# Putting float64 weights together as float32 with one multiplication and two bit operations

## The chip, the core and the metric

The kernel runs on one core of a Trainium2 chip. The metric is the device time of one execution in microseconds (us), the median of several runs. The core has five engines with a queue of instructions each, executed in the order of the program: TensorE (PE), VectorE (DVE), ScalarE (ACT), GpSimd (POOL) and SyncE (SP). DMA transfers run beside them.

## What is computed

The reference is an attention over a small state, a mixture of experts in which each row takes one expert, and a dense feed-forward layer (FFN) on the result:

```python
def _moe_ref(x, expert_emb, tau, w1, w2):          # x: 4352 rows (B*S+Ns rows of attention) of 512
    ...                                            # routing: expert_idx = argmax of cosine logits, gate_w = its softmax value
    for e in range(8):
        mask = expert_idx == e
        h = np.maximum(x[mask] @ w1[e], 0.0)       # w1[e]: 512 x 1024
        out[mask] = gate_w[mask, None] * (h @ w2[e])

def _moe2_ref(x, w_in, w_out):                     # w_in: 512 x 2048, w_out: 2048 x 512
    h = x @ w_in
    relu6 = np.clip(h + 3.0, 0.0, 6.0)
    g = h * relu6 / 6.0
    return (g @ w_out).astype(np.float32)
```

`w1` and `w2` come as float32. `w_in` and `w_out` are drawn as float32 and multiplied by `1.0 / np.sqrt(...)`, a float64 number, so they arrive as **float64**: each value is a pair of 32-bit words. The output is float32.

## The kernel before

The kernel splits every float32 operand of its large products into a high half, rounded to PE's float32r format, and a low half, what the rounding left; a product is then three matmuls (high by high, high by low, low by high). Four stretches follow one another, with overlap:

- **Attention**, up to some 130 us: eight batches, each with its scores, exponentials and products, whose results `xr` go to a DRAM buffer.
- **Routing**, to some 145 us: the logits `lg` of all rows, their argmax, a rank of each row within its expert, and from that the tiles (slots) of 128 rows.
- **Experts**: a lead part (a unit of four slots and a single one), then units of two slots and of one. For each, rows are fetched, transposed (`xq`) and split (`xt`); expert weights are loaded as `raw` and split into `wh` (a cast) and `wl` (a subtraction, L1249); `h_ps` is the first product (L1410), `hx` its split Relu, `y_ps` or `y_g` the second product (L1513); the result rows go to the DRAM buffer `ysd` by way of tiles `yt`.
- **FFN**: 17 blocks of 256 rows. A block's rows are read back and split into `yh` and `yw`; then sixteen times F1 (`u_ps`, L1619, weights `wih` and `wil`) and F2 (`o`, L1654, weights `woh` and `wol`). Between them `r` is a Relu on ACT with a bias of three (L1623), then a product with the smaller of `r` and 6 on DVE, and its split into `gh` and `gl`. At a block's end the two accumulators are scaled by 1/6 (L1668, L1670) and stored. Blocks of the FFN run among the expert units.

**The conversions.** The float64 weights become float32 in 32 conversions (`Conv`), one for every 128 x 512 chunk: sixteen chunks of `w_in` (m = 0 to 15, `i`) and sixteen of `w_out` (`o`). A chunk is loaded as pairs of words by a DMA that ACT issues; `low` and `top` are views of every second word of that buffer. Seven instructions follow: on ACT `cv` (L295), a Relu over the upper 16 bits of the lower word, that leaves a small integer in `low`; on DVE `ca` (L303, L304), which shifts the upper word and takes its sign and exponent bits together in `cv_m`; on ACT `cq` (L312), a Square of the upper word read as a float; on DVE `cb` (L308), which puts the small integer into the last bits, and `cp` (L316), which multiplies by zero where the square is below a bound; then the split, `ch` (L324, ACT, a copy into the high half) and `cl` (L327, the subtraction for the low half, on POOL or DVE).

The first 14 conversions take their buffers from a pool of their own (`cv_raw` and `cv_m`, two of each). The last 18 take the raw buffer from the FFN's tiles `yh` and `yw`, and `cv_m` from the pool of rows ("row", six buffers), which the tiles `yt` and the output rows use as well. In the trace such a conversion therefore reads `cv_m<-yh`.

**What sets the order.** A planner (`Sched`) runs while the program is built. Every step of the kernel is an operation with a cost for each engine, a due time (`prio`), the operations that it depends on, and the ring of buffers from which it takes (`hold`) and gives back. The planner appends, one after another, the operation that can begin earliest by its own reckoning, with the due time weighed in, and so fixes the order of every engine's queue. A conversion of an FFN weight is due 36.654 planner microseconds ahead of the F1 or F2 that first needs it (L1779 to L1786). In `convert` the raw buffer (`hr`) is taken by the load and `cv_m` (`hc`) by `ca`; both are given back after `cl`.

Of the kernel before, what the change touches and what calls it, by code (L numbers as in the profile page):

```python
# [8 lines left out]
F32 = mybir.dt.float32  # L9
F32R = mybir.dt.float32r  # L10
BF16 = mybir.dt.bfloat16
I32 = mybir.dt.int32
U16 = mybir.dt.uint16
AF = mybir.ActivationFunctionType
ALU = mybir.AluOpType
# [139 lines left out]
def kernel(  # L155
# [13 lines left out]
    PE, ACT, DVE, POOL, SP = nc.tensor, nc.scalar, nc.vector, nc.gpsimd, nc.sync  # L169
# [97 lines left out]
    class Conv:  # L267
# [4 lines left out]


        def __init__(self, w, m):
            self.w, self.m = w, m
            src = w_in if w == "i" else w_out
            self.wide = src.dtype != F32
            self.src, self.n = (src.bitcast(I32), 2) if self.wide else (src, 1)

        def load(self, pool):  # L280
# [7 lines left out]
            if self.wide:  # L288
                v = t.rearrange("p (f w) -> p f w", w=2)
                self.low, self.top = v[:, :, 0], v[:, :, 1]  # L290

        def cv(self):

            if self.wide:
                ACT.activation(self.low, self.raw.bitcast(U16).rearrange("p (f w) -> p f w", w=4)[:, :, 1], AF.Relu,  # L295
                               bias=seven[:, 0:1], scale=-(2.0**-13))

        def ca(self, pool):
            self.ma = self.raw
            if self.wide:  # L300
                t = self.bits = pool().bitcast(I32)
                self.ma = t.bitcast(F32)
                DVE.tensor_scalar(t, self.top, 3, 0x3FFFFFFF, op0=ALU.logical_shift_left, op1=ALU.bitwise_and)  # L303
                DVE.scalar_tensor_tensor(t, self.top, -0x40000000, t, op0=ALU.bitwise_and, op1=ALU.bitwise_or)  # L304

        def cb(self):
            if self.wide:
                DVE.scalar_tensor_tensor(self.bits, self.low, 7, self.bits, op0=ALU.bitwise_xor, op1=ALU.bitwise_or)  # L308

        def cq(self):  # L310
            if self.wide:
                ACT.activation(self.top.bitcast(F32), self.top.bitcast(F32), AF.Square)  # L312

        def cp(self, e="P"):
            if self.wide:
                eng[e].scalar_tensor_tensor(self.ma, self.top.bitcast(F32), (1.0625 * 2.0**-15)**2, self.ma,  # L316
                                            op0=ALU.is_ge, op1=ALU.mult)

# [11 lines left out]
    last_conv, dense = [None], {}  # L330

    def convert(n, prio, pool, ma, gate=None, start=0.0):

# [5 lines left out]
        a.ready = start  # L339
        v = op(c.cv, {"A": 0.55}, prio, [a])  # L340
        b = op(lambda: c.ca(ma), {"D": 0.96}, prio, [a], [hc], port="D")
        q = op(c.cq, {"A": 0.55}, prio, [b])
        b = op(c.cb, {"D": 0.61}, prio, [b, v], port="D")
        f = op(lambda: c.cp("D"), {"D": 0.6}, prio, [b, q], port="D")
        g = op(c.ch, {"A": 0.55}, prio, [f, home])
        dense[conv_q[n]] = op(*((lambda: c.cl("P"), {"P": 1.26}) if early else (c.cl, {"D": 0.6, "P": 1.26})), prio, [g], (), [hr, hc], port="DP")
        if early:
# [827 lines left out]
    pool = {}  # L1175
# [432 lines left out]
    def F1(i, m, prio, deps=()):  # L1608
# [12 lines left out]
        def ra():  # L1621
            q["r"] = pool["ffn"].tile([128, 256], F32, tag="r", name="r")
            ACT.activation(q["r"], q["p"], AF.Relu, bias=pool["three"][:, 0:1])  # L1623

# [17 lines left out]
    def F2(i, m, prio, deps=()):  # L1642
# [18 lines left out]
        for a in range(2):  # L1661
# [3 lines left out]
            def scale(a=a, box=box):  # L1665
                t = box["t"] = pool["row"].tile([128, W], F32, tag="row", name="yo")[:, 0:DM]
                if a:
                    DVE.tensor_scalar(t, o["o"][1], 1.0 / 6, None, op0=ALU.mult)  # L1668
                else:
                    ACT.activation(t, o["o"][0], AF.Copy, scale=1.0 / 6)  # L1670

# [201 lines left out]
```

## Time and profile before

| | |
|---|---|
| median of 3 runs | 1447.35 us |
| the runs | 1445.01, 1447.35, 1447.62 us |
| the profiled execution, its own time | 1445.17 us |
| its span (first to last instruction) | 1443.5 us |
| mean granted clock of TensorE | 0.961 of full speed |
| bytes read from and written to HBM | 146.09 MB, 27.82 MB |

The profile is of one execution of the program; its time lies within the runs. A page of it gives the busy time of each engine, and the same in 40 slices of the span (36 us each). Behind the page stands the trace, from which busy times of single stretches, waits with the instruction that ended them, and single instructions in order of time are read. PEclk is the TensorE clock that was granted, as a share of full speed: 1 is 2.4 GHz, 0.5 is 1.2 GHz. PE is the matmuls, PEld the weight loads that overlap them.

### The profile page before, as it was taken

What the parts mean: (1) busy time and instruction counts of PE and PEld (TensorE: products, weight loads), DVE (VectorE), ACT (ScalarE), POOL (GpSimd) and SP (SyncE); (2) the same over time, 40 slices, a digit from 0 to 9 for tenths busy, and PEclk for the clock granted to TensorE, in tenths of its full rate; (3) what the DMA queues carried; (4) which work ended last, traced back from release to release, by engine and by line L of the source; (5) the groups of instructions that cost most, each with busy time, mean ns of one, the idle gap of its engine ahead of it and who ended that gap; (6) DMA issues with size and microseconds to landing.
All of it is one profiled execution on the core that took longest, in us unless ns stands there. A gap on an engine that the chain in (4) does not pass through costs nothing. (4 is left out here: it accounts for less than half of the span.)

```text
span 1443.5 us, 24914 instructions
## 1 busy us (share of the span) xinstructions
PE 1349.8 (94%) x8912; PEld 1194.9 (83%) x8912; DVE 907.5 (63%) x2102; ACT 588.5 (41%) x1276; POOL 421.0 (29%) x445
## 2 busy tenths in 40 slices
PE   7985797877899999999999999999999999999997
PEld 5764676775789899888989898998989999899996
DVE  6987876978865555545555545777756676434332
ACT  4764524555433243433334343333434444323332
POOL 4432546313252241413133133333333311100000
PEclk8997788999899999999999999999999999999999
DMA  6654336556454333333324233554545544101000
GB/s 161 182 168 144 123 103 179 181 169 189 132 176 145 106 102 112 112 109 97 117 89 125 89 111 110 161 154 159 163 135 156 167 142 152 46 23 30 15 16 15
DMA packets 151762, 175.60 MB, mean 122 GB/s; under 512 B 43784, under 2 KB 116488, under 8 KB 150608
## 3 DMA queue, kind: packets, MB, share of 16 engines
q1 hardware_dynamic: 128544, 121.19, 28.0%
q0 software_dynamic: 12336, 35.99, 8.2%
q10 hardware_dynamic: 10752, 16.78, 3.6%
q8 instruction: 71, 1.16, 0.3%
q14 instruction: 59, 0.48, 0.1%
HBM read 146.09 MB, written 27.82 MB: 120 GB/s over the span
## 5 line engine op out<-in xcount | busy, mean ns | idle before, releaser
L1619 PE MATMUL u_ps<-yh,wih 128*128 128x256 f32 x1088 | 305.6, 281 | 1.0 <-PEq L1828 0.9
L1619 PE MATMUL u_ps<-yw,wih 128*128 128x256 f32 x1088 | 305.7, 281 | 0.5 <-DVE yw L1598 0.5
L1619 PE MATMUL u_ps<-yh,wil 128*128 128x256 f32 x1088 | 305.2, 281 | 0.0
L1623 ACT ACTIVATE r<-u_ps,three 128x256 f32<-128x256 f32 x272 | 129.0, 474 | 347.5 <-PE u_ps L1619 343.3
L1626 DVE SCALAR_TENSOR_TENSOR u_ps<-r,u_ps 128x256 f32<-128x256 f32 x272 | 116.4, 428 | 223.4 <-ACT r L1623 223.1
L1654 PE MATMUL o<-woh,gh 128*128 128x512 f32 x544 | 216.7, 398 | 1.6 <-DVE yo L1668 1.3
L1654 PE MATMUL o<-wol,gh 128*128 128x512 f32 x544 | 215.9, 397 | 0.0
L1619 PEld LDWEIGHTS u_ps<-yh,wih 128*128 128x128 f32 x1088 | 205.7, 189 | 10.8 <-DVE gl L1633 2.2
L1654 PE MATMUL o<-woh,gl 128*128 128x512 f32 x544 | 214.4, 394 | 0.0
L1619 PEld LDWEIGHTS u_ps<-yw,wih 128*128 128x128 f32 x1088 | 205.0, 188 | 8.7 <-DVE yw L1598 0.7
L1619 PEld LDWEIGHTS u_ps<-yh,wil 128*128 128x128 f32 x1088 | 205.6, 189 | 0.0
L1249 DVE TENSOR_TENSOR wl<-raw,wh 128x512 fp32r<-128x512 f32 x272 | 191.1, 712 | 9.2 <-ACT wh L1246 4.7
L1630 ACT CAST gh<-u_ps 128x256 fp32r<-128x256 f32 x272 | 101.3, 372 | 211.7 <-PE o L1654 168.7
L1633 DVE TENSOR_TENSOR gl<-u_ps,gh 128x256 fp32r<-128x256 f32 x272 | 114.8, 422 | 112.7 <-ACT gh L1630 112.3
L1513 PE MATMUL y_ps<-wh,hx 128*128 128x512 f32 x512 | 184.5, 397 | 0.0
L1249 POOL TENSOR_TENSOR wl<-raw,wh 128x512 fp32r<-128x512 f32 x80 | 109.5, 1369 | 252.2 <-DVE wh L1246 122.8
L1277 POOL DMA_INDIRECT xq<-xd,qidx x128 | 130.4, 1018 | 79.0 <-DVE xt L1330 44.0
L1410 PE MATMUL h_ps<-xt,wh 128*128 128x256 f32 x704 | 145.9, 297 | 0.8 <-ACT wh L1246 0.6
L1246 DVE CAST wh<-raw 128x512 fp32r<-128x512 f32 x232 | 100.6, 436 | 63.2 <-PE y_ps L1513 23.0
L1410 PE MATMUL h_ps<-xt,wl 128*128 128x256 f32 x352 | 105.6, 300 | 27.8 <-DVE wl L1249 23.0
L1673 POOL DMA_INDIRECT out_dram<-yo,ix x34 | 37.5, 1104 | 311.1 <-DVE yo L1668 215.7
L1410 PEld LDWEIGHTS h_ps<-xt,wh 128*128 128x128 f32 x704 | 122.3, 206 | 2.8 <-ACT wh L1246 0.8
(299 smaller groups left out, 2262.1 us busy)
## 6 DMA issues: line engine op xcount, KB each, us to landing
raw<-in_moe_w_dram SPq DMA_DIRECT2D x176, 512.0 KB, 3.9
yl<-ysd SPq DMA_DIRECT2D x136, 64.0 KB, 2.6
xd<-xr SPq DMA_DIRECT2D x8, 1056.0 KB, 4.8
ysd<-yt POOLq DMA_DIRECT2D x32, 256.5 KB, 3.1
xb<-in_x_dram SPq DMA_DIRECT2D x48, 128.0 KB, 3.1
yw<-in_moe_w_out_dram ACTq DMA_DIRECT2D x9, 512.0 KB, 4.0
cv_raw<-in_moe_w_in_dram ACTq DMA_DIRECT2D x8, 512.0 KB, 5.5
yh<-in_moe_w_in_dram ACTq DMA_DIRECT2D x8, 512.0 KB, 4.9
```

Source lines behind the costliest of these rows:

```text
L1246: copy[e](pc["hi"], box["t"][:, j, :])
L1249: eng[e].tensor_tensor(pc["lo"], box["t"][:, j, :], f32(pc["hi"]), op=ALU.subtract)
L1277: POOL.indirect_dma_start(q[:, j * QW:(j + 1) * QW], None, xd_q, index(qidx[:, j, s:s + 1]))
L1410: PE.matmul(out(f), pc[w][:, (2 * c + f) * 128:(2 * c + f + 1) * 128], u.xt[a][:, 2 * j + c, 256 * hf:256 * hf + 256], start=new and c == ...
L1513: PE.matmul(u.y[i], u.ht[t][:, a, lo + 128 * i:lo + 128 * i + 128], pc[w], start=c == 0 and k == 0, stop=c == KF - 1 and k == 2)
L1619: PE.matmul(p, w, y[:, k, :], start=k == 0 and j == 0, stop=k == KD - 1 and j == 2)
L1623: ACT.activation(q["r"], q["p"], AF.Relu, bias=pool["three"][:, 0:1])
L1626: DVE.scalar_tensor_tensor(q["p"], q["r"], 6.0, q["p"], op0=ALU.min, op1=ALU.mult)
L1630: ACT.copy(q["h"], q["p"])
L1633: DVE.tensor_tensor(q["l"], q["p"], f32(q["h"]), op=ALU.subtract)
L1654: PE.matmul(o["o"][a], g[:, a * 128:(a + 1) * 128], w, start=m == 0 and j == 0, stop=m == KFF - 1 and j == 2)
L1673: POOL.indirect_dma_start(out, bass.IndirectOffsetOnAxis(ap=o["ix"][:, a:a + 1], axis=0), box["t"], None)
```

## The change

A conversion is made of other instructions. ACT's `cv` stays and is followed by a second one, `cw`, which turns the small integer round (7 minus it) in place. ACT's `cg` multiplies the upper word, read as a float, by 2^-111, in place; the Square is gone. Of DVE's four instructions two are there: `ca` joins the sign bit of the upper word to the small integer, in place in the raw buffer; `cb` shifts the upper word by three and joins it, into `cv_m`. So the float32 weight is 256 times the weight; the FFN's Relu undoes that for `w_in` (a scale of 2^-8 at L1623, the bias of three as before), and the two output scales undo it for the product with the gate and for `w_out`.

In the planner `cv_m` is now taken by `cb`, and the raw buffer is given back by `cb`, not by `cl`. The costs that the planner reckons with are those of the new steps. All lines behind `Conv` move down by two or less (L1249 becomes L1251).

```diff
+        def cg(self):
+            if self.wide:
+                ACT.activation(self.top.bitcast(F32), self.top.bitcast(F32), AF.Copy, scale=2.0**-111)
+
         def cv(self):
...
+        def cw(self):
+            if self.wide:
+                ACT.activation(self.low, self.low, AF.Copy, bias=7.0, scale=-1.0)
+
+        def ca(self):
+            if self.wide:
+                DVE.scalar_tensor_tensor(self.low, self.top, -0x80000000, self.low, op0=ALU.bitwise_and, op1=ALU.bitwise_or)
+
-        def ca(self, pool):
+        def cb(self, pool):
             self.ma = self.raw
             if self.wide:
-                t = self.bits = pool().bitcast(I32)
+                t = pool().bitcast(I32)
                 self.ma = t.bitcast(F32)
-                DVE.tensor_scalar(t, self.top, 3, 0x3FFFFFFF, op0=ALU.logical_shift_left, op1=ALU.bitwise_and)
-                DVE.scalar_tensor_tensor(t, self.top, -0x40000000, t, op0=ALU.bitwise_and, op1=ALU.bitwise_or)
-
-        def cb(self):
-            if self.wide:
-                DVE.scalar_tensor_tensor(self.bits, self.low, 7, self.bits, op0=ALU.bitwise_xor, op1=ALU.bitwise_or)
-
-        def cq(self):
-            if self.wide:
-                ACT.activation(self.top.bitcast(F32), self.top.bitcast(F32), AF.Square)
-
-        def cp(self, e="P"):
-            if self.wide:
-                eng[e].scalar_tensor_tensor(self.ma, self.top.bitcast(F32), (1.0625 * 2.0**-15)**2, self.ma,
-                                            op0=ALU.is_ge, op1=ALU.mult)
+                DVE.scalar_tensor_tensor(t, self.top, 3, self.low, op0=ALU.logical_shift_left, op1=ALU.bitwise_or)
...
+    unit_i, unit_o = (1.0 if t.dtype == F32 else 2.0**-8 for t in (w_in, w_out))
...
-        v = op(c.cv, {"A": 0.55}, prio, [a])
-        b = op(lambda: c.ca(ma), {"D": 0.96}, prio, [a], [hc], port="D")
-        q = op(c.cq, {"A": 0.55}, prio, [b])
-        b = op(c.cb, {"D": 0.61}, prio, [b, v], port="D")
-        f = op(lambda: c.cp("D"), {"D": 0.6}, prio, [b, q], port="D")
+        v = op(c.cv, {"A": 0.66}, prio, [a])
+        v = op(c.cw, {"A": 0.57}, prio, [v])
+        b = op(c.cg, {"A": 0.57}, prio, [a])
+        b = op(c.ca, {"D": 0.61}, prio, [b, v], port="D")
+        f = op(lambda: c.cb(ma), {"D": 0.61}, prio, [b], [hc], [hr] if c.wide else (), port="D")
...
-            ACT.activation(q["r"], q["p"], AF.Relu, bias=pool["three"][:, 0:1])
+            ACT.activation(q["r"], q["p"], AF.Relu, bias=pool["three"][:, 0:1], scale=unit_i)
...
-                    DVE.tensor_scalar(t, o["o"][1], 1.0 / 6, None, op0=ALU.mult)
+                    DVE.tensor_scalar(t, o["o"][1], unit_i * unit_o / 6, None, op0=ALU.mult)
```

Since the planner reckons anew, the order of the queues changes in many places up to the second block of the FFN. Three of them stand here. In a row of the order the line comes first, then the operation, out<-in and the shape.

**First place: the routing's second scan.** On DVE, before the change, from the reciprocal `rs` of the state's softmax to the copies `lg` of the last batches' logits, the conversion stands among the latter:

```order
L605 RECIPROCAL rs<-rs 128x16
L671 COPY lg<-xr_ps 128x8
L672 TENSOR_TENSOR lg<-lg,xr_ps 128x8
L303 TENSOR_SCALAR cv_m<-cv_raw 128x512
L304 SCALAR_TENSOR_TENSOR cv_m<-cv_raw,cv_m 128x512
L308 SCALAR_TENSOR_TENSOR cv_m<-cv_raw,cv_m 128x512
L316 SCALAR_TENSOR_TENSOR cv_m<-cv_raw,cv_m 128x512
L671 COPY lg<-xr_ps 128x8
L672 TENSOR_TENSOR lg<-lg,xr_ps 128x8
```

After the change:

```order
L607 RECIPROCAL rs<-rs 128x16
L673 COPY lg<-xr_ps 128x8
L674 TENSOR_TENSOR lg<-lg,xr_ps 128x8
L309 SCALAR_TENSOR_TENSOR cv_raw<-cv_raw 128x512
L316 SCALAR_TENSOR_TENSOR cv_m<-cv_raw 128x512
L673 COPY lg<-xr_ps 128x8
L674 TENSOR_TENSOR lg<-lg,xr_ps 128x8
```

At the same place two instructions stand where four stood. On ACT before the change, from the state rows' copies `sxT` and `xrs` on, the Square stands behind the copies `xr` of the attention's results (one row stands for four of them):

```order
L690 COPY sxT<-sx_ps 128x512
L702 COPY xrs<-sx 128x4x64 x2
L664 COPY xr<-xr_ps 128x2x4x66 x4
L312 ACTIVATE cv_raw<-cv_raw 128x512
L324 CAST wih<-cv_m 128x512
L653 COPY ah<-a_ps 128x2x256
L295 ACTIVATE cv_raw<-cv_raw,seven 128x512
```

And after the change:

```order
L323 CAST wih<-cv_m 128x512
L300 ACTIVATE cv_raw<-cv_raw,seven 128x512
L295 ACTIVATE cv_raw<-cv_raw 128x512
L305 ACTIVATE cv_raw<-cv_raw 128x512
L692 COPY sxT<-sx_ps 128x512
L704 COPY xrs<-sx 128x4x64 x2
L598 ACTIVATE e_1559<-e_1559 128x512
L655 COPY ah<-a_ps 128x1024
L285 DMA cv_raw<-in_moe_w_in_dram 128x4x256
L666 COPY xr<-xr_ps 128x2x4x66 x4
L655 COPY ah<-a_ps 128x2x256
L323 CAST wih<-cv_m 128x512
```

The conversion's three ACT instructions (L300, L295, L305) stand ahead of `sxT` and of the four copies `xr` now; behind the copies stands only its last cast (L323).

**Second place: the lead expert's second layer.** On DVE before the change, after the transposes of the next unit's rows (`xt` is their split, `gates` a column of its gate values, `wl` a piece of an expert weight):

```order
L1330 TENSOR_TENSOR xt<-xq,xt 128x2x128 x4
L1358 TENSOR_SCALAR gates<-gates 128x1
L1359 RECIPROCAL gates<-gates 128x1
L303 TENSOR_SCALAR cv_m<-cv_raw 128x512
L304 SCALAR_TENSOR_TENSOR cv_m<-cv_raw,cv_m 128x512
L308 SCALAR_TENSOR_TENSOR cv_m<-cv_raw,cv_m 128x512
L316 SCALAR_TENSOR_TENSOR cv_m<-cv_raw,cv_m 128x512
L1249 TENSOR_TENSOR wl<-raw,wh 128x512
L303 TENSOR_SCALAR cv_m<-cv_raw 128x512
L304 SCALAR_TENSOR_TENSOR cv_m<-cv_raw,cv_m 128x512
L1249 TENSOR_TENSOR wl<-raw,wh 128x512
```

After the change:

```order
L1317 STREAM_TRANSPOSE xq<-xq 128x4x64 x4
L1332 TENSOR_TENSOR xt<-xq,xt 128x2x128 x4
L1251 TENSOR_TENSOR wl<-raw,wh 128x512
L309 SCALAR_TENSOR_TENSOR cv_raw<-cv_raw 128x512
L1251 TENSOR_TENSOR wl<-raw,wh 128x512
L316 SCALAR_TENSOR_TENSOR cv_m<-cv_raw 128x512
L1251 TENSOR_TENSOR wl<-raw,wh 128x512
L309 SCALAR_TENSOR_TENSOR cv_raw<-cv_raw 128x512
```

The `wl` stands ahead of the conversion instead of behind it, and the instructions between the following `wl` are single ones.

**Third place: the rows of the third pair of slots**, with the conversions whose raw buffers are `yw` and `yh`, on DVE before the change:

```order
L1315 STREAM_TRANSPOSE xq<-xq 128x4x64 x4
L303 TENSOR_SCALAR cv_m<-yw 128x512
L304 SCALAR_TENSOR_TENSOR cv_m<-yw,cv_m 128x512
L308 SCALAR_TENSOR_TENSOR cv_m<-yw,cv_m 128x512
L1330 TENSOR_TENSOR xt<-xq,xt 128x2x128 x4
L316 SCALAR_TENSOR_TENSOR cv_m<-yw,cv_m 128x512
L303 TENSOR_SCALAR cv_m<-yh 128x512
L304 SCALAR_TENSOR_TENSOR cv_m<-yh,cv_m 128x512
L308 SCALAR_TENSOR_TENSOR cv_m<-yh,cv_m 128x512
L316 SCALAR_TENSOR_TENSOR cv_m<-yh,cv_m 128x512
L1249 TENSOR_TENSOR wl<-raw,wh 128x512
```

After the change:

```order
L1328 CAST xt<-xq 128x2x128 x2
L1332 TENSOR_TENSOR xt<-xq,xt 128x2x128 x2
L309 SCALAR_TENSOR_TENSOR yw<-yw 128x512
L316 SCALAR_TENSOR_TENSOR cv_m<-yw 128x512
L1332 TENSOR_TENSOR xt<-xq,xt 128x2x128 x2
L1635 TENSOR_TENSOR gl<-u_ps,gh 128x256
L309 SCALAR_TENSOR_TENSOR yh<-yh 128x512
L316 SCALAR_TENSOR_TENSOR cv_m<-yh 128x512
L326 TENSOR_TENSOR wol_2790<-cv_m,woh_2789 128x512
L326 TENSOR_TENSOR wil_2792<-cv_m,wih_2791 128x512
L1251 TENSOR_TENSOR wl<-raw,wh 128x512
```

The two conversions and the splits `xt` stand in nearly the same order with half the instructions; the low halves `wol` and `wil` of FFN weights (L326) and a `gl` have come ahead of the `wl`.

## Rows read from the trace of the kernel before

**Rows 1.** The page: busy time of each engine; busy tenths of PE in 40 slices.

```profile
PE 1349.8 (94%) x8912; PEld 1194.9 (83%) x8912; DVE 907.5 (63%) x2102; ACT 588.5 (41%) x1276; POOL 421.0 (29%) x445
PE   7985797877899999999999999999999999999997
```

**Rows 2.** Busy us by stage: PE, PEld, DVE, ACT, POOL (instructions), PEclk, DMA share, GB/s.

```profile
36.00:108.00 72.00, 66.47 (x793) 51.13 (x791) 61.90 (x126) 52.31 (x87) 27.34 (x41) 1.00 0.59 175
108.00:144.00 36.00, 21.40 (x178) 17.35 (x178) 27.14 (x85) 15.93 (x27) 7.86 (x12) 0.79 0.39 141
144.00:252.00 108.00, 88.78 (x481) 75.18 (x482) 83.44 (x217) 47.59 (x107) 56.76 (x55) 0.80 0.47 136
252.00:397.00 145.00, 115.88 (x647) 101.53 (x647) 123.47 (x253) 77.38 (x156) 40.85 (x39) 0.89 0.54 168
433.00:1443.50 1010.50, 996.91 (x6370) 898.72 (x6368) 564.51 (x1307) 368.66 (x845) 252.83 (x243) 0.99 0.35 106
```

**Rows 3.** Waits, 252 to 397 us: engine, line, releaser, us, times, longest.

```profile
PE h_ps L1410 <- DVE wl L1249: 20.5, 6, 5.8
ACT yh L312 <- DVE cv_m L304: 13.1, 8, 3.1
PE y_ps L1513 <- DVE wl L1249: 7.2, 2, 6.7
...
DVE wh L1246 <- DMA raw<-in_moe_w_dram: 4.6, 3, 2.6
...
PE h_ps L1410 <- ACT wh L1246: 0.6, 1, 0.6
```

**Rows 4.** PE in time: start, us, instruction [us idle before it <- releaser].

```profile
228.93 0.79 PE L1513 MATMUL y_g<-wl,hx 128*128 128x512 f32 x1 [3.31 <-DVE wl L1249]
...
311.19 0.58 PE L1410 MATMUL h_ps<-xt,wl 128*128 128x256 f32 x1 [5.81 <-DVE wl L1249]
...
336.46 0.80 PE L1513 MATMUL y_ps<-wl,hx 128*128 128x512 f32 x1 [6.68 <-DVE wl L1249]
```

**Rows 5.** DVE in time ahead of the wait at 311.19.

```profile
303.17 0.43 DVE L303 TENSOR_SCALAR cv_m<-yw 128x512 int32<-128x512 int32 x1 [3.89 <-DMA ysd<-yt]
...
307.89 0.69 DVE L316 SCALAR_TENSOR_TENSOR cv_m<-yh,cv_m 128x512 f32<-128x512 f32 x1
...
310.46 0.67 DVE L1249 TENSOR_TENSOR wl<-raw,wh 128x512 fp32r<-128x512 f32 x1
```

**Rows 6.** DVE in time ahead of the wait at 228.93.

```profile
225.62 0.41 DVE L303 TENSOR_SCALAR cv_m<-cv_raw 128x512 int32<-128x512 int32 x1
...
228.20 0.68 DVE L1249 TENSOR_TENSOR wl<-raw,wh 128x512 fp32r<-128x512 f32 x1
```

**Rows 7.** A conversion's instructions: ns min/median/max, first and last start, forms.

```profile
L303 DVE TENSOR_SCALAR cv_m<-yh x9: 420/427/1400, 263.1 to 379.1; 128x512 int32<-128x512 int32 x9
L304 DVE SCALAR_TENSOR_TENSOR cv_m<-yh,cv_m x9: 691/692/694, 263.6 to 379.6; 128x512 int32<-128x512 int32 x9
L316 DVE SCALAR_TENSOR_TENSOR cv_m<-yh,cv_m x9: 669/693/693, 268.8 to 381.1; 128x512 f32<-128x512 f32 x9
L295 ACT ACTIVATE yh<-yh,seven x9: 753/761/786, 257.9 to 371.2; 128x512 int32<-128x512 uint16 x9
L312 ACT ACTIVATE yh<-yh x9: 679/689/712, 264.3 to 380.3; 128x512 f32<-128x512 f32 x9
L324 ACT CAST wih<-cv_m x16: 617/620/624, 49.5 to 360.9; 128x512 fp32r<-128x512 f32 x16
```

**Rows 8.** Busy us of instructions on `cv_m`, 252 to 397: DVE, ACT, POOL.

```profile
252.00:397.00 145.00, 56.86 (x89) 11.14 (x18) 1.30 (x1) 0.89 0.54 168
```

**Rows 9.** Routing: a conversion's last instruction on DVE, and a PE transpose, in time.

```profile
127.58 0.69 DVE L316 SCALAR_TENSOR_TENSOR cv_m<-cv_raw,cv_m 128x512 f32<-128x512 f32 x1 [2.21 <-ACT cv_raw L312]
...
128.69 0.63 PE L647 MATMUL a_ps<-ident,e 128*128 128x128 f32 x4 [1.90 <-DVE lg L671]
```

**Rows 10.** Conversions begun on DVE from 36 to 108 us, columns as in rows 7.

```profile
L303 DVE TENSOR_SCALAR cv_m<-cv_raw x5: 415/417/459, 44.3 to 106.5; 128x512 int32<-128x512 int32 x5
```

More of the change, by code (lines that the diff above doesn't have):

```diff
@@ L339, in convert @@
         a.ready = start
-        v = op(c.cv, {"A": 0.55}, prio, [a])
-        b = op(lambda: c.ca(ma), {"D": 0.96}, prio, [a], [hc], port="D")
-        q = op(c.cq, {"A": 0.55}, prio, [b])
-        b = op(c.cb, {"D": 0.61}, prio, [b, v], port="D")
-        f = op(lambda: c.cp("D"), {"D": 0.6}, prio, [b, q], port="D")
+        v = op(c.cv, {"A": 0.66}, prio, [a])
[3 more added lines that the diff above has]
+        f = op(lambda: c.cb(ma), {"D": 0.61}, prio, [b], [hc], [hr] if c.wide else (), port="D")
         g = op(c.ch, {"A": 0.55}, prio, [f, home])
-        dense[conv_q[n]] = op(*((lambda: c.cl("P"), {"P": 1.26}) if early else (c.cl, {"D": 0.6, "P": 1.26})), prio, [g], (), [hr, hc], port="DP")
+        dense[conv_q[n]] = op(*((lambda: c.cl("P"), {"P": 1.26}) if early else (c.cl, {"D": 0.6, "P": 1.26})), prio, [g], (),
+                              [hc] if c.wide else [hr, hc], port="DP")
         if early:
@@ L1667, in scale @@
                 if a:
-                    DVE.tensor_scalar(t, o["o"][1], 1.0 / 6, None, op0=ALU.mult)
+                    DVE.tensor_scalar(t, o["o"][1], unit_i * unit_o / 6, None, op0=ALU.mult)
                 else:
-                    ACT.activation(t, o["o"][0], AF.Copy, scale=1.0 / 6)
+                    ACT.activation(t, o["o"][0], AF.Copy, scale=unit_i * unit_o / 6)
             def put(a=a, box=box):
```

## The prediction, made before the changed kernel ran

> **What bounds the kernel now.** I began with the page's busy shares and slices. TensorE (PE) is busy 94% of the span and VectorE (DVE) 63%, and from the thirteenth of the 40 slices on nearly every PE slice reads 9; before that they read 5 to 9 [rows 1]. So this kernel has two halves. The busy times by stage say it in numbers: from 433 us to the end PE is busy 996.9 of 1010.5 us at a granted clock of 0.99, and nothing that shortens another engine's work can help there. From 252 to 397 us it is the other way round: PE is busy 115.9 of 145 us at a granted clock of 0.89, while DVE is busy 123.5 [rows 2]. That stretch is where the last 18 of the 32 conversions of the float64 weights run (the first 14 are spread over 36 to 252 us).
>
> Next the waits inside that stretch. PE stood 20.5 us and 7.2 us for `wl`, the low half of an expert weight, made by DVE (L1249); almost nothing else held it up [rows 3]. The third look is at what DVE did ahead of those `wl`. PE had waited 6.68 us at 336.46 and 5.81 us at 311.19 [rows 4]. Ahead of the latter DVE had stood 3.89 us at the first instruction of a conversion (L303), because `cv_m` takes a buffer of the row pool that a store was still reading; then two conversions ran, the last of their eight instructions from 307.89, and the `wl` that PE wanted started at 310.46 [rows 5]. At 228.93 PE had waited 3.31 us [rows 4], and a whole conversion stood straight ahead of the `wl`, from 225.62 to 228.20 [rows 6]. The queues are executed in program order, so a conversion in front of a `wl` is time that PE pays. All time saved before 433 us reaches the end, as PE is full from there on and the order of PE's queue is the same before and after the change from about 400 us of the old trace.
>
> **DVE: four instructions per conversion become two.** Removed are L303 (427 ns at the median), L304 (692), L308 (692, the form of L304) and L316 (693); added are two scalar_tensor_tensor of the same 128x512 size [rows 7]. The first of the two writes every second word in place, which no DVE row shows. Its bounds are 0.69 us, the price of the forms that read that stride, and twice that, 1.39; I take 0.69, since L304 and L308 have it whether one or both sources are strided. That saves 0.42 + 3 x 0.69 - 2 x 0.69 = 1.11 us per conversion: 20.0 us for the 18 of the 252 to 397 us stretch. As a cross-check, DVE instructions on `cv_m` there last 56.9 us for 89 instructions [rows 8]; less the 17 of L327 that stay, at the 0.69 of the two-source forms, 45.1 us for 72, against 36 x 0.69 = 24.8 afterwards: 20.3.
>
> The order of the queue takes some of it back. Between the first and the second block of the FFN rows on DVE the program now has 5 more casts `wh`, 2 more `wl`, 1 more `hx` and 2 casts `xt`, less 2 `yh` and 1 `wol`: 3.4 us at 0.43, 0.69, 0.69, 0.41, 0.43 and 0.69 us. The three prices not shown among the rows are of the size of those that are (a one-source form about 0.43, a two-source form 0.69). Net 16.9 us. DVE also waited 4.6 us there for expert weights to land [rows 3]; that does not shrink, and grows first when DVE comes sooner, so I take 16.9 - 4.6 = 12.3 us as what reaches PE. The lower bound is 5: the third place of the order (above) is one where the `wl` still gets two whole conversions and part of other work ahead of it, so at several places nothing may move, and the one at 311 alone gives 2 x 1.11. The upper bound is 20.3 + 3.9 = 24, with the wait for the row buffer gone too: the buffer is now asked for by the second instruction, not the first, and is held for a shorter time.
>
> **Routing, 108 to 144 us.** Ahead of the second routing scan DVE had a conversion whose last instruction waited 2.21 us for ScalarE's Square (L312), which stood behind ScalarE's copies of `xr`; PE's transposes waited 1.90 us for the `lg` copy behind it [rows 9]. In the first place of the order the two new instructions still stand there, but their ScalarE work is queued ahead of those copies. I take 1.9 us, from 0 to 4 (the whole 2.21 wait and two instructions less, on a chain where DVE hands to PE and back).
>
> **Second layer of the lead expert, 225 to 229 us.** The second place of the order has the `wl` ahead of the conversion now. The conversion's 2.58 us in front of it go [rows 6]; of the 3.31 us wait I take 2.6, from 0 (the raw weights land no sooner) to 3.3.
>
> **The attention stage, 36 to 108 us.** DVE is busy 61.9 of 72 us, but PE 66.5 at full clock [rows 2]. Five conversions [rows 10] save 5.6 us of DVE time beside a PE that is nearly full: 0 to 3 us, I take 0.
>
> **TensorE's clock.** The granted 0.89 in 252 to 397 us means 22% of it, 32 us, at 1.2 GHz, the rest at 2.4 [rows 2]. The low stretches follow PE's waits. Of 28 us of waits 12.3 go, some 45%. If all 32 us were work at half speed, 16 us would be lost and 7 come back; much of the low time is the waits themselves. I take 2, from 0 to 7.
>
> **ScalarE: three instructions become four.** Removed is Square (L312, 689 ns); added are two Copy with constants. Their nearest rows are the copy L324 (620 ns) and L295 (761 ns), so 0.62 to 0.76; I take 0.62, since the added forms are copies, one of them on the float32 words that Square took. The sum per conversion is +0.55 us, 18 us over all 32. ScalarE is busy 77 of 145 us in the stage [rows 2], so the cover is its idle time, part of which was a wait for DVE: 13.1 us at the Square of `yh` alone, which goes with the Square [rows 3]. But queued behind these copies stand `wh`, `hx`, `r` and `gh`, which PE's operands pass through. I take 1.5 us lost, from 0 to 18 x 1.24 = 22 us. The scales put into L1623, L1668 and L1670 are constants of instructions that are there anyway: nothing.
>
> **Loads.** The raw buffer is given back at the second DVE instruction instead of after the subtraction L327, so the next load is issued earlier. That feeds the conversions faster (no credit taken); DMA engines are busy 0.54 of the stage [rows 2]. SP's queue keeps its order but for a few row loads.
>
> **The sum.** 12.3 + 1.9 + 2.6 + 0 + 2 - 1.5 = 17.3 us. The profiled execution took 1445.2 us (its span 1443.5 and 1.7 around it); it becomes 1427.9. The median of the runs shown, 1447.35, is 2.2 above it, so I expect a median of about 1430.
>
> **Whether the busiest engine rule speaks against this.** Rows 1 put PE at 94% and DVE at 63% of the span, rows 2 put DVE ahead of PE in one stage. The Trainium skill (Perfetto Trace Analysis, Identifying the Most-Contended Engine) says to optimise the engine of highest occupancy first, with LDWEIGHTS busy as TensorE's measure; by the whole span that is TensorE (83% by weight loads), and the sum would be 0, by the stage it is DVE, and the sum is the one above. The page's next section, Optimization Strategy, allows that the most contended engine changes over time; the trace agrees, since rows 2 show it change at about 400 us.
>
> **Rivals.** (a) Nothing measurable: PE is the bound everywhere, DVE's shorter work only turns into DVE idle time. For it: 94% over the span. Against it: 20.5 + 7.2 = 27.7 us of PE waiting for `wl` in one stage. It gives about 1447. The page just named stands for this reading. (b) What is next in line takes half: raw expert weights land when they land (4.6 us waited there already), `hx` casts and row buffers come late; then the stage gives its lower 5 us and no clock, with 1.9 and 0 elsewhere: about 1445.2 - 5.4 + 2.2 = 1442. (c) Slower: in ScalarE's queue three instructions now run as one block as soon as a load lands, so a `wh`, `gh` or `hx` behind them comes up to 1.24 us later (two copies). It decides once PE's waits end at ScalarE rather than DVE; if every one of the 18 late conversions costs PE that much, 22 us are lost against 17 to 19 gained elsewhere, about 1451. Against it: ScalarE is half idle there and PE waited 0.6 us for it in all [rows 3]. (d) The strided in-place write costs 1.39 us: the saving per conversion falls to 0.42, the stage gives 3, the rest 1.9 + 2.6 - 1.5 = 3: 1447.4 - 6, about 1441.
>
> **How the numbers follow.** Forecast 70%, 1411 to 1440; (b) 10%; (d) 5%; (a) 8%; (c) 7%. The median of this kernel can be told from no change at about 0.2%, 2.9 us: faster is then the forecast, (b) and (d), 85%; the same 8%; slower 7%. The range that leaves out (a), (c) and the far end of the bounds is 1410 to 1444.
>
> **What would show it.** Right: DVE busy some 35 us less over the span (32 x 1.11), the two new lines near 0.69 us each, PE's waits for `wl` in the stretch and at 228.93 down from 31 to about 16 us, the granted clock of that stretch nearer 1, and PE full from about 415 instead of 433 us. Wrong: PE waits for ScalarE casts of several us (c); DVE idle grown as much as its work shrank, with PE's waits unchanged (a); waits for raw loads ahead of each `wl` (b); a new line above 1 us (d).

## The result, and the profile after the change

The changed kernel takes **1425.35 us** (median of four runs, 1423.14 to 1427.65) beside 1446.18 us of the kernel before (1444.37 to 1447.62). The ratio is 0.9857, with a 95% interval from 0.9836 to 0.9877: faster by 20.8 us. The prediction was 1430, from 1410 to 1444, with faster at 0.85. The profiled execution is the longest of the four, 1427.65 us with a span of 1426.0 (1443.5 before), so a comparison of the two traces explains 17.5 us and not all of the 20.8.

The page first, as in [rows 1]: busy time of each engine, and PE's busy tenths in 40 slices.

```profile
PE 1340.8 (94%) x8912; PEld 1184.8 (83%) x8912; DVE 867.1 (61%) x2037; ACT 606.6 (43%) x1313; POOL 414.7 (29%) x441
PE   7985797968999999999999999999999999999997
```

DVE has 40.4 us less work (907.5 before; the prediction had some 35), ACT 18.1 more (588.5 before). The share of PE is the same 94%, but the last slice below 9 (ahead of the end) is the tenth instead of the eleventh. By stage, with the columns of [rows 2]:

```profile
36.00:108.00 72.00, 66.66 (x798) 51.77 (x797) 55.75 (x121) 56.62 (x95) 25.44 (x41) 1.00 0.59 175
108.00:144.00 36.00, 19.56 (x174) 15.40 (x173) 26.68 (x82) 19.08 (x34) 13.43 (x16) 0.82 0.51 169
144.00:252.00 108.00, 92.33 (x517) 78.23 (x516) 74.45 (x203) 50.95 (x113) 56.03 (x55) 0.85 0.47 145
252.00:397.00 145.00, 122.53 (x716) 106.67 (x715) 109.59 (x245) 86.70 (x181) 42.08 (x44) 0.94 0.59 176
433.00:1420.00 987.00, 978.57 (x6266) 882.41 (x6265) 554.47 (x1281) 365.68 (x841) 245.87 (x236) 1.00 0.34 104
```

From 252 to 397 us PE has 716 matmul rows where it had 647, DVE is now the less busy engine of the two, and the granted clock went from 0.89 to 0.94.

**Where the time was gained.** The same stretch of time holds other work after the change, so I counted work instead: every matmul at one fixed duration for its kind (that of the full stretch behind 433 us), summed in PE's order. The table says when PE had done the work that, in the kernel before, it had done by a given time. The last two columns are of an experiment below, the kernel without `cw`.

| before, us | changed kernel, us | gained | `e14_no_cw_plan_again`, us | gained |
|---|---|---|---|---|
| 160 (the lead expert's first layer begins) | 155.8 | 4.2 | 155.4 | 4.6 |
| 232 (within its second layer) | 223.8 | 8.2 | 221.2 | 10.8 |
| 280 | 271.4 | 8.6 | 268.5 | 11.5 |
| 360 | 350.6 | 9.4 | 339.7 | 20.3 |
| 433 | 415.6 | 17.4 | 399.0 | 34.0 |
| 1443.5 (end of the span) | 1426.0 | 17.5 | 1410.4 | 33.1 |

All of it is gained ahead of 433 us, and what is gained there reaches the end: 17.4 and 17.5. Half of that, 8.6, is gained ahead of 280 us. One execution of a kernel differs from the next, so two more traces belong beside the table. At its first five times the changed kernel's second profiled execution (`e13_after_again`, 1422.35 us) has gained 3.3, 8.0, 9.7, 12.3 and 20.4 us, and that of `e8_no_cw_plan` (1422.24 us), the same kernel as the last column on another chip, 4.7, 9.0, 7.9, 16.1 and 25.5. So what the table gives for a stretch is known to some 2 us for the changed kernel, and to 5 for the one without `cw`.

The conversion's instructions, with the columns of [rows 7] (duration in ns, lowest, median and highest):

```profile
L300 ACT ACTIVATE yh<-yh,seven x9: 748/775/789, 253.9 to 359.1; 128x512 int32<-128x512 uint16 x9
L295 ACT ACTIVATE yh<-yh x9: 640/667/682, 254.8 to 359.8; 128x512 f32<-128x512 f32 x9
L305 ACT ACTIVATE yh<-yh x9: 635/657/670, 255.4 to 360.4; 128x512 int32<-128x512 int32 x9
L309 DVE SCALAR_TENSOR_TENSOR yh<-yh x9: 687/693/697, 256.2 to 362.6; 128x512 int32<-128x512 int32 x9
L316 DVE SCALAR_TENSOR_TENSOR cv_m<-yh x9: 683/693/694, 257.1 to 364.4; 128x512 int32<-128x512 int32 x9
```

Both of DVE's instructions take 0.69 us, the one that writes every second word in place (L309) like the other. ACT's two added ones take 0.66 and 0.67 us.

PE's waits from 252 to 397 us, and three of DVE's, as in [rows 3] (us in total, times, longest):

```profile
PE u_ps L1621 <- DVE gl L1635: 6.9, 2, 6.5
PE h_ps L1412 <- DVE wl L1251: 5.9, 6, 2.0
PE u_ps L1621 <- DVE yt L1539: 4.9, 1, 4.9
PE y_ps L1515 <- DVE wl L1251: 3.5, 3, 1.7
...
DVE yh L309 <- ACT yh L305: 5.1, 7, 1.3
DVE yw L309 <- ACT yw L305: 4.6, 5, 1.6
DVE wh L1248 <- DMA raw<-in_moe_w_dram: 4.1, 3, 1.6
```

The waits for `wl` fell from 27.7 to 9.4 us. DVE's wait for expert weights to land stays (4.6 before, 4.1 now). Two things are new. PE waits 11.8 us at the first matmul of an F1 (L1621); the 4.9 of them that are put down to `yt`, a copy of one column, may well be for the `gl` straight ahead of it in DVE's queue, which ran from 350.12 to 350.54, PE from 350.60. And DVE stands 9.7 us at L309 for ACT's `cw` (L305); before, a conversion's first instruction on DVE needed only the load, and no wait of this kind was among its waits.

### The profile page after: what moved, and what is told of

Read it like the earlier page. It is cut to its first block, busy times and chain, and to the rows that moved or that the text cites. A ratio compares the mean times of both kernels' runs of the same rounds, so it can differ in the third digit from the quotient of the medians.

```text
span 1426.0 us, 24825 instructions
## 1 busy us (share of the span) xinstructions
PE 1340.8 (94%) x8912; PEld 1184.8 (83%) x8912; DVE 867.1 (61%) x2037; ACT 606.6 (43%) x1313; POOL 414.7 (29%) x441
## 5 line engine op out<-in xcount | busy, mean ns | idle before, releaser
L1621 PE MATMUL u_ps<-yh,wih 128*128 128x256 f32 x1088 | 308.3, 283 | 17.0 <-DVE gl L1635 6.9
L1621 PE MATMUL u_ps<-yw,wih 128*128 128x256 f32 x1088 | 307.9, 283 | 0.1
L1621 PE MATMUL u_ps<-yh,wil 128*128 128x256 f32 x1088 | 307.3, 282 | 0.0
L1621 PEld LDWEIGHTS u_ps<-yh,wih 128*128 128x128 f32 x1088 | 207.9, 191 | 27.3 <-ACT yh L295 6.9
L1621 PEld LDWEIGHTS u_ps<-yw,wih 128*128 128x128 f32 x1088 | 207.4, 191 | 8.4 <-DVE yw L1600 0.4
L1621 PEld LDWEIGHTS u_ps<-yh,wil 128*128 128x128 f32 x1088 | 208.0, 191 | 0.0
L1251 DVE TENSOR_TENSOR wl<-raw,wh 128x512 fp32r<-128x512 f32 x277 | 194.0, 711 | 8.5 <-ACT wh L1248 3.8
L1251 POOL TENSOR_TENSOR wl<-raw,wh 128x512 fp32r<-128x512 f32 x75 | 103.9, 1385 | 229.1 <-DVE wh L1248 121.7
L1412 PE MATMUL h_ps<-xt,wh 128*128 128x256 f32 x704 | 136.7, 283 | 1.8 <-DVE wh L1248 1.8
L1656 PEld LDWEIGHTS o<-woh,gl 128*128 128x128 f32 x544 | 102.1, 188 | 24.9
L1656 PEld LDWEIGHTS o<-woh,gh 128*128 128x128 f32 x544 | 102.2, 188 | 19.6 <-DVE yo L1670 2.2
```

What stands on the lines that cost most here:

```text
L1251: eng[e].tensor_tensor(pc["lo"], box["t"][:, j, :], f32(pc["hi"]), op=ALU.subtract)
L1412: PE.matmul(out(f), pc[w][:, (2 * c + f) * 128:(2 * c + f + 1) * 128], u.xt[a][:, 2 * j + c, 256 * hf:256 * hf + 256], start=new and c == ...
L1621: PE.matmul(p, w, y[:, k, :], start=k == 0 and j == 0, stop=k == KD - 1 and j == 2)
L1656: PE.matmul(o["o"][a], g[:, a * 128:(a + 1) * 128], w, start=m == 0 and j == 0, stop=m == KFF - 1 and j == 2)
```

## The experiments

All are variants of the changed kernel unless the text says otherwise, and a ratio is to the kernel before on the same chip. Differences in us against the changed kernel use its second measurement (`e13_after_again`, 1425.69 us, ratio 0.9864, interval 0.9840 to 0.9888). `e1` to `e4` ran on another chip than that one, where the kernel before took 1444.71 us beside 1444.72; for `e7` to `e10`, on a third one (1448.80), the ratios are compared.

**VectorE's instructions twice, in an unchanged order.**

```diff
-                DVE.scalar_tensor_tensor(self.low, self.top, -0x80000000, self.low, ...)
+                for _ in range(2):
+                    DVE.scalar_tensor_tensor(self.low, self.top, -0x80000000, self.low, ...)
...
-                DVE.scalar_tensor_tensor(t, self.top, 3, self.low, ...)
+                for _ in range(2):
+                    DVE.scalar_tensor_tensor(t, self.top, 3, self.low, ...)
```

> The changed kernel with both of VectorE's new instructions of every conversion issued twice (the second time they write the same values again), the order of all queues unchanged: 32 x 1.38 us more work on VectorE, somewhat more than the 32 x 1.11 us that the change took away. Theory (the gain is VectorE's time ahead of what TensorE waits for): of the 20.8 us gained, 20.8 x 1.38 / 1.11 = some 26 come back at most, as much as 15 at least: 1440 to 1451 us. Rival (the gain comes from the planner's new order, the instructions matter little): at most 5 us, 1425 to 1430 us.

Measured: 1465.10 us, ratio 1.0126 (1.0098 to 1.0155). 44.2 us of DVE work (32 x 1.38) cost 39.4 us, 0.9 for each, and the kernel is slower than before the change. That is more than either expectation had.

The same with `range(2 if conv.index(self) >= NCE else 1)`, that is, in the last 18 conversions only:

> As the run with both VectorE instructions twice, but only for the last 18 conversions (from 252 us on). Theory (by the terms of the prediction some 12 of 17 us came from these): 12.3 x 1.38 / 1.11 = 15 us more, 1437 to 1444 us. Rival (the gain came ahead of them, from routing and the lead expert): at most 6 us more, 1425 to 1431 us.

Measured: 1454.70 us, ratio 1.0061 (1.0037 to 1.0085). 24.8 us of work cost 29.0, more than its length; by the table's way of counting, the changed kernel and this one are even up to 232 us (8.2 and 7.7 gained) and 23 us apart at 360. So most of what added DVE work costs lies in the late conversions (29.0 of 39.4 us), and the rival, at most 6 us, falls. It does not follow that the gain lies there: by the table half of it came ahead of 280 us. Both runs cost more than the theory had, and in both the planner did not know of the added work. So:

```diff
-        b = op(c.ca, {"D": 0.61}, prio, [b, v], port="D")
-        f = op(lambda: c.cb(ma), {"D": 0.61}, prio, [b], [hc], ...)
+        b = op(c.ca, {"D": 1.22}, prio, [b, v], port="D")
+        f = op(lambda: c.cb(ma), {"D": 1.22}, prio, [b], [hc], ...)
```

> The changed kernel with both of VectorE's instructions of a conversion twice, as before, but with the planner told so (1.22 us where 0.61 stood, twice). Theory (VectorE's time in the first 430 us is worth nearly its full length, whatever the order): of the 39.8 us that this cost in the old order most stay, 1455 to 1468 us. Rival (as with ScalarE, where a new order took half of it back): some 20 us, 1440 to 1450 us.

Measured: 1443.24 us, ratio 0.9983 (0.9968 to 0.9998). The theory fell: with an order made for it, the same 44.2 us cost 17.6 us, not 39.4. Work that the order does not expect costs twice as much here as work that it does; 7 of the 22 us between the two runs are lost in one stretch behind 433 us, which the run without `cw` comes back to. This run also says what the gain is made of. The conversions' instructions on DVE last 83.9 us before the change and 45.8 after it; with somewhat more work put back than the 38.1 us that went, all else as in the changed kernel, the time is within 0.2% of the kernel before. DVE's shorter conversions are the gain, or nearly all of it.

**ScalarE's `cw` three times**, which gives the same integer.

```diff
-                ACT.activation(self.low, self.low, AF.Copy, bias=7.0, scale=-1.0)
+                for _ in range(3):
+                    ACT.activation(self.low, self.low, AF.Copy, bias=7.0, scale=-1.0)
```

> The changed kernel with ScalarE's cw (7 minus the integer) issued three times, which gives the same integer: 32 x 1.32 us more work on ScalarE, at the same places of the same order. Theory (ScalarE has room and its extra instruction costs next to nothing): 0 to 5 us more, 1425 to 1430 us. Rival (ScalarE's block ahead of the casts that TensorE needs is what is late now): 18 x 1.32 = 24 us more from the late conversions alone, some 1449 us.

Measured: 1457.07 us, ratio 1.0074 (1.0055 to 1.0093): 31.4 us for 42.2 us of ScalarE work. The theory that ScalarE has room fell. By the table's count, against the changed kernel's first trace, 7 of the 31 us are lost ahead of 108 us, 15 between 232 and 433 us and 7 up to 600. For the late conversions, DVE's longest waits from 252 to 397 us (`cw` is L306 there and `ca` L310) show one way that it takes:

```profile
DVE yh L310 <- ACT yh L306: 16.6, 9, 2.8
DVE yw L310 <- ACT yw L306: 11.5, 8, 2.2
```

DVE stood 28.1 us at `ca`, against 9.7 in the changed kernel, and everything behind `ca` in DVE's queue stood with it. That is another way than the one of the rival in the prediction, casts behind ScalarE's block. Work behind the block is late too, in the attention stage: from 36 to 108 us PE waits 6.9 us for ScalarE in this kernel, against 1.7 in the changed one. With the planner told of it (1.71 us for `cw`):

> The changed kernel with cw three times, and the planner told so (1.71 us where 0.57 stood). Theory (the work itself costs): most of the 31.7 us stay, 1448 to 1460 us. Rival (VectorE stands at ca only because the order was made for a shorter ScalarE chain): 1440 us or less.

Measured: 1444.64 us, ratio 0.9968 (0.9955 to 0.9981), on a chip where the kernel before took 1448.80. That is 0.0104 above the changed kernel's ratio, 15 us: again about half, and between the two expectations. DVE's two waits at `ca` come to 12.8 us there instead of 28.1.

**ScalarE's `cw` taken out.** `cv` rounds to the integer directly, so a conversion has three ScalarE instructions, as before the change.

```diff
         def cv(self):
-                ACT.activation(self.low, ..., AF.Relu, bias=seven[:, 0:1], scale=-(2.0**-13))
+                ACT.activation(self.low, ..., AF.Copy, bias=-0.5, scale=2.0**-13)
...
         def cw(self):
-                ACT.activation(self.low, self.low, AF.Copy, bias=7.0, scale=-1.0)
```

> The changed kernel with ScalarE's cw taken out and cv put as one Copy (the halfword times 2^-13 less 0.5, rounded to an integer from 0 to 7), so that a conversion has three ScalarE instructions as before the change; VectorE's work and the order of the rest as in the changed kernel. By the run with cw three times, 42 us of ScalarE work cost 31.7 us, 0.75 us for each; theory (this holds the other way too, ScalarE's added instruction gives back part of VectorE's gain): 32 x 0.66 x 0.75 = 16 us less, 1405 to 1414 us. Rival (only work that the planner doesn't know of hurts, and ScalarE's block as it stands is hidden): 0 to 5 us less, 1420 to 1426 us.

Measured: 1433.03 us, ratio 0.9895 (0.9864 to 0.9925). Against the changed kernel's 0.9864 that is no gain, and the two intervals overlap: the theory that the cost of added work holds the other way fell for an order that is left as it is. The trace shows 18.0 us gained by 433 us, between the changed kernel's two traces (17.4 and 20.4), and then 7 lost up to 600. DVE's waits at `ca` fell to 4.1 us, yet PE's waits at F1 stayed, 10.9 us for 11.8:

```profile
PE u_ps L1621 <- DVE yt L1539: 5.7, 1, 5.7
PE u_ps L1621 <- DVE gl L1635: 5.2, 2, 5.0
```

So in that order ScalarE's `cw` is not what PE's new waits come from. Part of the loss behind 433 us begins here (ACT's `r`, and PE before and after it):

```profile
422.23 0.47 ACT L1625 ACTIVATE r<-u_ps,three 128x256 f32<-128x256 f32 x1 [8.37 <-PE u_ps L1621]
...
418.08 0.28 PE L1621 MATMUL u_ps<-yh,wil 128*128 128x256 f32 x1
...
423.55 0.50 PE L1515 MATMUL y_ps<-wh,hx 128*128 128x512 f32 x1 [2.42 <-DVE wh L1248]
```

`r` needs the F1 whose last matmul started at 418.08, yet starts at 422.23; the `wh` that PE then lacks stands behind DVE's use of `r`. Why `r` started 3.9 us after that matmul's end the trace does not show. The kernels with `cw` three times and with DVE's work twice lose about as much in that stretch, the changed kernel does not. That stays open.

With the step taken out of the planner too:

```diff
-        v = op(c.cw, {"A": 0.57}, prio, [v])
```

> As the run without cw, with the step taken out of the planner too, so that the queues are ordered for the shorter conversions. Theory: as that run or up to 6 us less, 1400 to 1414 us. Rival (the planner moves other work into the room, as at the casts between the first two blocks): 1415 us or more.

Measured: 1416.83 us, ratio 0.9771 (0.9741 to 0.9801): the rival's side, and yet faster than the changed kernel. Beside the changed kernel on one chip:

> The changed kernel as it is, on the chip of the runs beside it: 0.983 to 0.988 of the kernel before. It is what the next two are compared with.

> The kernel without cw and ordered for that, again, beside the changed kernel on one chip. Theory (ScalarE's added instruction costs some 12 us of what VectorE gains): 0.974 to 0.980 of the kernel before, 8 to 14 us under the changed kernel. Rival (the difference came from comparing chips): within 4 us of it.

Measured: 1425.69 us, ratio 0.9864, and **1410.49 us**, ratio 0.9758 (0.9741 to 0.9775). The kernel without `cw` is 15.2 us faster than the changed kernel and 34.2 faster than the one before; it beats both. That is a little more than the 8 to 14 us expected. The two kernels differ in two things, the step and the order. Its PE waits and DVE's waits at `ca` (L305 there) from 252 to 397 us:

```profile
PE y_ps L1510 <- DVE wl L1246: 5.0, 4, 3.0
PE h_ps L1407 <- DVE wl L1246: 3.4, 3, 1.8
...
PE u_ps L1616 <- DVE gl L1630: 0.2, 1, 0.2
...
DVE yh L305 <- ACT yh L295: 2.4, 2, 1.4
...
DVE yw L305 <- ACT yw L295: 1.5, 3, 0.8
```

The waits for `wl` are as in the changed kernel (8.4 us), DVE's at `ca` fell from 9.7 to 3.9, and of the 11.8 us at F1 0.2 are left.

**ScalarE's part before the change.** The kernel before, without its Square:

```diff
         def cq(self):
-                ACT.activation(self.top.bitcast(F32), self.top.bitcast(F32), AF.Square)
```

> The kernel before with ScalarE's Square left out of the conversions (the comparison that follows reads the word as it is, so negative weights become zero); VectorE's work and all orders as in the kernel before. Theory (ScalarE's part of a conversion was on the path already): 32 x 0.69 x 0.75 = 17 us less, 1424 to 1434 us. Rival (ScalarE hidden, as the prediction had it, but for the wait at the Square in routing): 2 to 5 us less, 1440 to 1443 us.

Measured: 1444.35 us beside 1448.80, ratio 0.9967 (0.9945 to 0.9990): 4.8 us for 22 us of ScalarE work. That is 0.2 us for each us, where `cw` three times cost 0.7 in the changed kernel. Here ScalarE was nearly hidden, as the 0.6 us that PE waited for it said [rows 3]; with the change, added ScalarE work no longer is.

**The planner's side of the change.** First the costs of DVE in the planner as they were (0.96 and 1.21 us), with the new instructions:

```diff
-        b = op(c.ca, {"D": 0.61}, prio, [b, v], port="D")
-        f = op(lambda: c.cb(ma), {"D": 0.61}, prio, [b], [hc], ...)
+        b = op(c.ca, {"D": 0.96}, prio, [b, v], port="D")
+        f = op(lambda: c.cb(ma), {"D": 1.21}, prio, [b], [hc], ...)
```

> The changed kernel, but the planner reckons with VectorE's costs of the kernel before (0.96 and 1.21 us where 0.61 and 0.61 stood), so that the order of the queues is close to one made for the longer conversions; the instructions are the new ones. Theory (the work itself is the gain): three quarters of it or more stay, 1425 to 1430 us. Rival (the order is the gain): 1436 us or more.

Measured: 1429.92 us (1428.83 to 1439.70), ratio 0.9895 (0.9878 to 0.9911), 4 us above the changed kernel, with intervals that overlap. Most of the gain is the work; that the order for the shorter steps adds a fifth is likely and not shown. Then the buffers as the planner held them before:

```diff
-        b = op(c.ca, {"D": 0.61}, prio, [b, v], port="D")
-        f = op(lambda: c.cb(ma), {"D": 0.61}, prio, [b], [hc], [hr] if c.wide else (), port="D")
+        b = op(c.ca, {"D": 0.61}, prio, [b, v], [hc], port="D")
+        f = op(lambda: c.cb(ma), {"D": 0.61}, prio, [b], port="D")
...
-                              [hc] if c.wide else [hr, hc], port="DP")
+                              [hr, hc], port="DP")
```

> The changed kernel, with the planner's ring of buffers as before the change: cv_m is taken at ca and the raw buffer is given back after cl, so that loads stand later in the order. Instructions as in the changed kernel. Theory (the change's gain is engine time; no credit was taken for earlier loads): within 4 us of the changed kernel. Rival (earlier loads feed the conversions and carry part of the gain): 5 to 12 us above it.

Measured: 1419.62 us, ratio 0.9830 (0.9810 to 0.9850). Neither came: the old holds are 6 us better than the new ones on the same chip (by the ratios 5, and the two intervals overlap by 0.001). The new holds are no part of the gain; the order that follows from them seems to cost something. By the table's count this kernel, with all four ScalarE instructions, has gained 8.5 us at 280 and 23.6 at 433: 15.1 us in the late stretch, where the changed kernel's two traces have 8.8 and 10.7. DVE's waits at `ca` are 2.6 us in it. So part of what the kernel without `cw` gains can be had by another order with `cw` in place. The old holds together with the kernel without `cw` were not tried.

## Why the prediction was right, point by point

**The bound and the place.** Right. PE had waited for `wl` behind conversions in DVE's queue, the waits fell from 27.7 to 9.4 us (the prediction left some 16, with the one at 228.93), and what was gained ahead of 433 us reached the end. With DVE's work put back and the order made for it, all but some 2 us of the gain went. The reading by the whole span (the Trainium skill, Perfetto Trace Analysis, Identifying the Most-Contended Engine) would have given no gain, since PE was the busiest engine and none of its work was touched; the measurement went with the reading by stage. Rival (a) fell with that, and (d) with L309's 693 ns.

**Routing and attention**, 1.9 us predicted, 4.2 found at 160 us (3.3 in the second trace). In the changed kernel the conversion's two instructions at the place that was named no longer wait for ACT.

```profile
120.89 0.69 DVE L309 SCALAR_TENSOR_TENSOR cv_raw<-cv_raw 128x512 int32<-128x512 int32 x1
121.61 1.42 DVE L316 SCALAR_TENSOR_TENSOR cv_m<-cv_raw 128x512 int32<-128x512 int32 x1
```

The 2.21 us of [rows 9] are gone, and with them PE's 1.90; PE has two waits of 0.74 us for ScalarE's copies `ah` instead. The place was half of it. PE's product `rk_ps` of the first scan started at 118.19 us before and 116.43 after, that of the second at 136.23 and 132.04. So 2.4 us were gained between the two, near the 1.9 of the prediction, and 1.8 already ahead of the first, for which the prediction had taken nothing.

**The lead expert's second layer**, 2.6 us predicted, 4.0 found between 160 and 232 us. That is more than the whole wait of 3.31 us, because before the change the clock went with it: from 227.7 to 234.5 us it was granted at 0.50, and a `y_g` matmul that takes 0.40 us took 0.63. The `wl` stands ahead of the conversion (the last two lines of the second place of the order), and PE's wait of 3.31 us is 0.22:

```profile
221.51 0.69 DVE L1251 TENSOR_TENSOR wl<-raw,wh 128x512 fp32r<-128x512 f32 x1
...
222.25 0.50 PE L1515 MATMUL y_g<-wl,hx 128*128 128x512 f32 x1 [0.22 <-DVE wl L1251]
```

**The stage of the late conversions.** Short, and with that the total is luck in part. Predicted were 12.3 us from DVE, 2 from the clock and 1.5 lost to ScalarE, 12.8 together; the traces show 17.4 - 8.6 = 8.8 between 280 and 433 us of before, and 10.7 in the second one. Ahead of 280 us the prediction had 1.9 + 2.6 = 4.5 us, and the traces show 8.6 and 9.7. A late part that was too large and an early part that was too small make up for one another, and 17.3 meets the 17.5 of the trace (20.8 by the medians). A slip in the sum changes little: the work that the order adds comes to 3.5 us by the prices that are given, not 3.4.

How the stage divides between DVE and ScalarE is not shown. In the kernel without `cw` the same stretch gives 34.0 - 11.5 = 22.5 us (17.6 in the trace of `e8_no_cw_plan`). If the step were the only difference, ScalarE's fourth instruction would take back 12 to 14 us and not 1.5. But the order differs too. With `cw` out and the old order nothing was gained, and with `cw` in and the old holds the stretch gives 15.1. So `cw` costs something between nothing and 14 us in the stage, by the order that it stands in, and DVE's shorter work with its clock is worth up to 22.5 where 14.3 was taken. All of this lies within the bounds that were given (5 to 24 with a clock of up to 7; 0 to 22). (The kernel without `cw` also has a `cv` that is 0.09 us shorter, 3 us of ScalarE in all, which is counted with `cw` here.)

**ScalarE's cover** was the weakest step. The 1.5 us had no working: cover was read from the share of busy time (77 of 145 us) and from PE's waits, 0.6 us. But the change also moved ScalarE ahead of DVE: L303 had needed the load alone, `ca` needs the load and three ScalarE instructions in a row. A wait at `ca` holds up all that stands behind it in DVE's queue, and the prediction counted no such wait; the changed kernel has 9.7 us of them, 28.1 with `cw` three times. That ScalarE's work is not covered is shown by that run, 31.4 us for 42.2 (15 with an order made for it). What the one step of the change costs is not shown. Rival (c) had the right engine, and in the late stretch another way: it watched `wh`, `gh` and `hx` behind the block. The Square that the change removed had cost 4.8 us in all, so 689 ns removed against two copies added was no measure either. The prediction also took the planner's order as a term of 3.4 us; kernels with the same instructions and another order differ by some 5 us here.

**What is next late.** Rival (b) came in part, and by another instruction than those it named. With `wl` early, PE waits at F1 for the low half `gl`, which stands behind other work in DVE's queue as `wl` did. ACT's cast `gh`, DVE's queue up to the `gl` that needs it, and PE, in order of time:

```profile
312.44 0.36 ACT L1632 CAST gh<-u_ps 128x256 fp32r<-128x256 f32 x1
...
313.45 0.69 DVE L316 SCALAR_TENSOR_TENSOR cv_m<-yh 128x512 int32<-128x512 int32 x1
...
317.09 0.69 DVE L309 SCALAR_TENSOR_TENSOR yw<-yw 128x512 int32<-128x512 int32 x1
317.82 0.69 DVE L316 SCALAR_TENSOR_TENSOR cv_m<-yw 128x512 int32<-128x512 int32 x1
...
319.10 0.42 DVE L1635 TENSOR_TENSOR gl<-u_ps,gh 128x256 fp32r<-128x256 f32 x1
...
319.66 0.55 PE L1621 MATMUL u_ps<-yh,wih 128*128 128x256 f32 x1 [6.47 <-DVE gl L1635]
```

`gl` could have run at 312.8 and ran at 319.1; F1 needs the PSUM buffer that it frees. This is the third place of the order, where `gl` came ahead of the `wl` but behind a whole conversion and the end of another. DVE stood idle only 0.48 us in these 6.3 us, and not for `cw`; three of its instructions there, 2.1 us, are of conversions, the others are a low half `wil`, an `hx`, and transposes and splits of rows. So this wait comes from the order. It is not in the kernel without `cw` and its own order, it stays without `cw` in the old order, and in the kernel with the old holds PE waits 1.7 us for `gl` at F1.

**The clock.** For the same work, before, in the changed kernel and in the one without `cw`, with the columns of [rows 2]:

```profile
280.00:433.00 153.00, 125.48 (x716) 110.74 (x715) 122.58 (x271) 76.58 (x160) 48.29 (x50) 0.90 0.55 170
```

```profile
271.40:415.60 144.20, 121.46 (x710) 105.33 (x709) 106.84 (x245) 82.22 (x171) 42.40 (x45) 0.94 0.62 184
```

```profile
268.50:399.00 130.50, 119.39 (x710) 103.65 (x709) 107.01 (x240) 72.63 (x155) 47.34 (x49) 0.96 0.68 207
```

PE stood idle 27.5, 22.7 and 11.1 us, and was busy 125.5, 121.5 and 119.4 us with the same matmuls at a granted clock of 0.90, 0.94 and 0.96. So of the 8.8 us 4.8 are waits and 4.0 shorter matmuls, which goes with the clock that came back: 2 was predicted, within 0 to 7.

## What to carry to other kernels

An engine that is half idle can still hold up the path: ask which instruction of another engine's in-order queue waits for the last of its steps, and what stands behind that instruction. Where a planner fixes the order, the order is a term of its own. A saved step may pay nothing until the order is made for it (`cw` taken out: nothing measurable in the old order, 15 us in a new one) or pay most of its worth without that (DVE's, with the old costs in the planner), and a step that the planner doesn't know of cost twice (39 against 18 us). A run that undoes one term changes the order as well once the planner is told; only with a run that changes the order alone beside it does the difference say what the term is worth. And a total that comes out right says little for its terms.

## What was not expected of the hardware

- A VectorE instruction that reads and writes every second 32-bit word in place (L309) took 693 ns, the same as one that writes a whole tile (L316, 693 ns). No row of before showed it; of its bounds, 0.69 and 1.39 us, the prediction had taken the lower.
- ScalarE's copies over every second word took 657 and 667 ns, the cast of a whole tile of the same count 620 [rows 7]; 620 was predicted for both.
- ScalarE's `r` started 3.9 us after the end of the matmul that it needs in the kernel with `cw` taken out of the old order; the trace names no other cause.
